# Fixed step patterns, earlier k turns and spread loads in a threshold-attention kernel followed by a tanh-shrink layer

## The chip, the cores and the metric

The kernel runs on one core of a Trainium2 chip. The metric is device time in microseconds (us), lower is better. A core has TensorE (PE in the profile, matmuls), VectorE (DVE), ScalarE (ACT), GpSimd (POOL) and SyncE (SP, which here issues nearly all transfers). Each engine works off its own instructions in order and waits on semaphores for the others. PSUM is the memory that PE writes; only DVE and ACT read it here.

## The reference

```python
# q, k, v: 8 batches x 8 heads x 576 rows x 64, float32; tau = 0.02
scores = scale * np.matmul(q, k.transpose(0, 1, 3, 2))
thresh = np.max(scores, axis=-1, keepdims=True) - tau
scores = np.where(scores >= thresh, scores, -1000000000.0)
attn = softmax(scores)                   # written out in the reference
attn_out = np.matmul(attn, v)
x = attn_out.transpose(0, 2, 1, 3).reshape(4608, 512)
h = x @ w_in                             # 512 x 2048
out = (h - np.tanh(h)) @ w_out           # 2048 x 512
```

## The kernel before

**Pairs, tiles, slots.** Two heads of one batch make a pair p (32 pairs, 0 to 31; four pairs are a batch). A pair has nine tiles of 128 query rows (288 in all). One loop over a slot number s, from -8 to 292, writes the whole program: slot s issues the scores of tile s + 8, the threshold of tile s + 5, the exponentials of tile s and the value products of tile s - 2, so that every tile passes through all engines over some ten slots. Nothing reorders the code afterwards. The order of the loop is the order on each engine.

**What a slot holds.** On PE: the scores `psS` (two matmuls of 512 columns and two of 64, lines 322 and 331), then in some slots a layer step, in every odd slot the value products `psO` (lines 425, 432, 443), and what the plan adds. On DVE: the copy `sc` out of the scores with the row maximum (341), in every second slot `nb` (353), then `g` (517), `rc` and `osb` (457 to 463, the division by the sum), `xT` and `xR` (488, 489). On ACT: `z` (368), `th` (511, the tanh), and in every second slot `pT` (404, the exponential for two tiles). From pair 6 on the transposition between `z` and `pT` is a DMA, `zT`, issued by SP in every even slot (line 375); before that it is done on PE (`psZ`, 387).

**Layer steps.** When a batch is done, its 512 main rows go through the layer in a stage: 16 h steps (`psH`, four matmuls of 512 columns against w_in, line 498) and 16 y steps (`psY`, four matmuls of 512 columns against w_out, line 524; four parts make one output tile, copied out by `yo`, line 537, and stored by SP). Stage m runs beside the attention of batch m + 1, in the 36 slots from slot 36(m + 1) + 4; the last, for batch 6, has 32. `layers` makes the list of steps, and a running share spreads it evenly over `room`, the slots without a turn of k: 32 steps in 32 slots. Two stages follow after the last slot, at one step after another. The first stage has 16 h steps and 3 y steps.

**Turns and loads (the plan).** k and q of a pair are loaded as float32 (`kraw`, `qraw`, `vraw`; two DMAs each), split on POOL into two halves (`khl`, `qhl`), and turned: nine PE transposes into PSUM (`ps_k`, `ps_q`, line 240) and a copy by DVE (`kT`, `qT`, line 263). For k, POOL then copies the halves crosswise into `kS` (two copies of 64 x 1152, line 269), which the scores need as well. From pair 8 on q of three pairs in four is turned by a DMA instead (`qT<-qhl`, line 252). `PREP` says how many slots ahead of the pair's first scores (which are issued in slot 9p - 8) each of these stands. From pair 5 on k is turned six slots ahead for odd p and three for even p, in a slot that has no layer step. Loads of k, q and v stand in three slots in a row.

**PSUM.** `ps_big` has two buffers of two banks each, shared in turn by the scores of every tile and by the turns `ps_k` and `ps_q`: the third such tile has to wait until the first is copied out. `ps_h` has two buffers (h steps, `psX`), `ps_y` one (`psY`), `ps_o` one (`psO`).

Of the kernel before, what the change touches and what calls it, by code (L numbers as in the profile page):

```python
# [9 lines left out]
F32 = mybir.dt.float32  # L10
# [8 lines left out]
def kernel(  # L19
# [12 lines left out]
    P = 128  # L32

    B, H, S, D = q.shape
# [11 lines left out]
    HPAIR = H // 2  # L46
    NPAIR = B * HPAIR
# [4 lines left out]
    TPP = 9  # L52
    NTILE = NPAIR * TPP
# [9 lines left out]
    AHEAD = 8  # L63
    LDK = 16
# [61 lines left out]
    ps_big = pool("ps_big", 2, space=PSUM)  # L126
    ps_o = pool("ps_o", 1, space=PSUM)
# [108 lines left out]
    def turn_chunk(out, c, lhsT):  # L236
# [4 lines left out]
            out=out, lhsT=lhsT, rhs=rhs, is_transpose=True, start=True, stop=True  # L241
        )

    def q_by_dma(p):

        return p >= 2 * HPAIR and p % 4 != 0
# [49 lines left out]
    scs, mxs, nbs, zs, zts, pts, ops = {}, {}, {}, {}, {}, {}, {}  # L296

    def kind(i):

        return "AB"[i % 2]  # L300

    def place(i):

        p, j = divmod(i, TPP)
        j = j - p % 2
        return (p, None, 4) if j in (-1, 8) else (p, j // 4, j % 4)
# [102 lines left out]
    def attend(i):  # L409

        if kind(i) == "A":
            return
        p, hh, t = place(i)
        vb, pt = vbs[p % NV], pts[i]
        if hh is None:

            attend_shared(p - 1, 0, pt)
            return
        if t == 1:
            ops[p, hh] = ps_o.tile([P, 6, D + 1], F32, name="psO", tag="o")  # L420
            if p % 2 and hh == 0:
                attend_shared(p, 1, pts.pop(i - 2))
        po = ops[p, hh]

        nc.tensor.matmul(  # L425
            out=po[:, t - 1 : t + 1, :], lhsT=pt[:, 4 * P : 5 * P],
            rhs=vb[:, hh, 4:6, :], start=True, stop=False, skip_group_check=True,
        )
        for n in range(8):
            ab, c = divmod(n, 4)  # L430
            blk = 5 * ab + c
            nc.tensor.matmul(  # L432
                out=po[:, t - 1 + ab, :], lhsT=pt[:, blk * P : (blk + 1) * P],
                rhs=vb[:, hh, c, :], start=False, stop=(n == 7), skip_group_check=True,
            )
        pts.pop(i)
# [70 lines left out]
    def bend():  # L507
        while halves:
            m, n, ps = halves.pop(0)
            th = t_pool.tile([P, MB], F32, name="th")  # L510
            nc.scalar.activation(out=th, in_=ps, func=ACT.Tanh)  # L511
            ths.append((m, n, ps, th))
# [40 lines left out]
    EARLY = lambda m: 3 if m else 3  # L553
    LAST = 1

    FIRST = 3
    quarters = lambda m: [(m, ms, part) for ms in range(4) for part in range(4)]

    def layers(m, tail):


        def h_step(n):
            if tail and n % 2:
                ps = ps_big.tile([P, MB], F32, name="psHt", tag="big")
            else:
                ps = ps_h.tile([P, MB], F32, name="psH", tag="h")
            hidden(m, n, ps)

        def y_step(m, ms, part):
            if part == 0:  # L570

                odd = tail and (m, ms) > (B - 2, 1) and ms % 2 == 0
                pl, tag = (ps_o, "o") if odd else (ps_y, "y")
                ys[m, ms] = pl.tile([P, d_model], F32, name="psY", tag=tag), odd
            ps, odd = ys[m, ms]
            project(m, ms, part, ps, odd)

        def y_half(h):

            n = d_model // 2  # L580
            pl, tag = ((ps_y, "y"), (ps_o, "o"))[h]
            ps = pl.tile([P, n], F32, name="psY", tag=tag)
            for part in range(4):
                project(m, 3, part, ps, h == 0, slice(h * n, h * n + n))

        now = quarters(m - 1)[EARLY(m - 1) :] if m > 0 else []
        if m < NMB - 1:
            now += quarters(m)[: EARLY(m)]
        else:
            now += quarters(m)[:12]  # L590
        n = 16 + len(now)


        ahead = n - max(0, EARLY(m) - 3) - LAST if m < NMB - 1 else n - 9 - LAST
        steps, at, i = [], [], 0

        def ready(y):
            last = 4 * y[2] + 3
            return y[0] < m or len(at) > (last if m else 15) and at[last] + 2 < i

        while now or len(at) < 16:
            if len(at) < 16 and (
                not now or not ready(now[0]) or len(at) * ahead <= i * 16
            ) and not (m == B - 1 and i < FIRST):
                steps.append(lambda a=len(at): h_step(a))
                at.append(i)
            elif ready(now[0]):
                steps.append(lambda y=now.pop(0): y_step(*y))
            else:
                steps.append(lambda: None)  # L610
            i += 1
        if m == NMB - 1:
            steps += [lambda h=h: y_half(h) for h in range(2)]
        return steps
# [44 lines left out]
    for p in range(1, NPAIR):  # L659
        first = TPP * p - AHEAD  # L660
        for d, f in PREP[3 if p == 1 else 0 :]:
            d -= p == 1 and d in (3, 5)
            if d in (7, 8) and q_by_dma(p):
                d = d + 2
            if p in (2, 4):
                d = {8: 9, 7: 8, 5: 6}.get(d, d)
            elif d == 5 and p >= 5:
                d = 6 if p % 2 else 3
            plan.setdefault(first - d, []).append(lambda p=p, f=f: f(p))
        d = 7 if q_by_dma(p) else 3 - (p == 1 or p >= 5)  # L670
        d = 4 if p in (2, 4) else d
        plan.setdefault(first - d, []).append(lambda p=p: turn(p, "q"))

# [14 lines left out]
    todo, stage = [], 0  # L688
# [4 lines left out]
            plan.setdefault(-AHEAD, []).extend(plan.pop(at))  # L693

    turns = set()
    for p in range(HPAIR + 1, NPAIR):
        d = 6 if p % 2 else 3
        turns.add(TPP * p - AHEAD - (d if p >= 5 else 5))  # L700

    kinks, wts, atts = {}, {}, {}
    for i in range(NTILE + 3):
        at = i - 4 if i < HPAIR * TPP else i
# [4 lines left out]
    for s in range(-AHEAD, NTILE + LAG + 3):  # L709
        p, j = divmod(max(s, 0), TPP)  # L710
        if 0 <= s < NTILE and j == 2 + LAG and p % HPAIR == 0 and p >= HPAIR:
            assert not todo
            todo = layers(stage, False)
            room = range(s, min(s + HPAIR * TPP, NTILE))
            if room[-1] + 1 < NTILE:
                room = [a for a in room if a not in turns]
            share = len(todo) / len(room)
            done, stage = 0.0, stage + 1
        if s == NTILE:
            todo = layers(stage, True)  # L720
            share, done, stage = 1, 0.0, stage + 1
        if 0 <= s + AHEAD - 1 < NTILE:
            shift(s + AHEAD - 1)

        n = s + AHEAD
        if 0 < n < NTILE and place(n)[1] is None and kind(n) == "B":
            scores(n - 1)
        if 0 <= n < NTILE and (place(n)[1] is not None or kind(n) == "B"):
            scores(n)
        if s == 1 - AHEAD:  # L730
            for t in ("k", "q", "ks"):
                turn_first(t, 1)
        for i in kinks.pop(s, []):
            kink(i)
        bend()
        for i in wts.pop(s, []):
            weights(i)
        if 0 <= s < NTILE + FIRST:
            if todo and (s >= NTILE or s in room):
                done += share  # L740
                if s < NTILE and s == room[-1]:
                    done = 1e9
                while todo and done >= 1:
                    todo.pop(0)()
                    done -= 1
        if s == 0:
            nc.vector.tensor_tensor(
                out=fold, in0=ident_bf[:, 0:64], in1=ident_bf[:, 64:P], op=ALU.add
            )
        shrink()  # L750
        for store in stores[:-1]:
            store()
        del stores[:-1]
        for i in atts.pop(s, []):
            pp, jj = divmod(i, TPP)
            if i < NTILE:
                attend(i)
                odd = pp % 2
                if jj == 3 + odd:
                    norm(pp, 0)  # L760
                elif odd and jj in (0, 8):
                    norm(pp - (jj == 0), 1)
            if pp and jj == 1 + pp % 2:
                emit_x(pp - 1)
        for step in plan.pop(s, []):
            step()
        if s + AHEAD in cast_when:
            w_cast()
        if s + AHEAD in load_when:
            w_load(next(pieces))  # L770

    for step in todo:
        step()
        bend()
        shrink()
        for store in stores:
            store()
        stores.clear()
# [10 lines left out]
    _ = bass_utils  # L789
# [35 lines left out]
```

## Time and profile before

| | |
|---|---|
| median of 3 runs | 531.35 us (531.02 to 531.88) |
| the profiled execution's own time | 532.69 us |
| its span, first to last instruction | 530.9 us |
| busy: PE, ACT, DVE, POOL | 507.7, 433.4, 422.1, 289.3 us |
| TensorE clock granted | 1.0 of full speed throughout |
| DMA queue of SP | 85.56 MB, 77.4% of 16 engines' span |

The profile comes from one execution. A row of the timeline has the start in us, the duration, the engine and line, the operation with the tile it writes and those it reads, and in brackets how long the engine had stood idle before it and whose instruction ended that. Matmul ends are modelled: a row of PE ends about 0.16 us after the next one can start, so that a hole in PE is about that much longer than the idle time in brackets.

### The profile page before, as it was taken

How to read it: one execution, taken by the hardware profiler on the slowest of the kernel's cores; microseconds unless marked ns; L12 is line 12 of the kernel's file. 1: busy time of each engine (PE TensorE's matmuls, PEld its weight loads, DVE VectorE, ACT ScalarE, POOL GpSimd, SP SyncE). 2: the span in 40 equal slices, each digit the busy share in tenths (PEclk: the TensorE clock that was granted, in tenths of full speed). 3: DMA queues.
4: the chain of work that ended last, by engine and by line, in shares of the span. 5: the costliest groups of instructions: out<-in, count | busy, mean ns of one | idle time of the engine just before them, and what ended most of it. 6: DMA issues, size and time to landing. Idle time of an engine off the chain costs nothing.

```text
span 530.9 us, 12707 instructions
## 1 busy us (share of the span) xinstructions
PE 507.7 (96%) x4606; PEld 286.4 (54%) x4606; DVE 422.1 (80%) x1179; ACT 433.4 (82%) x617; POOL 289.3 (54%) x390
## 2 busy tenths in 40 slices
PE   8999899989999989999999999999999999999996
PEld 4666566554555545555555555555555555444444
DVE  5999889997898878998889888888899887554440
ACT  5999999998898989988998989899998989544330
POOL 7999999684738366574738383846657430000000
PEclk9999999999999999999999999999999999999999
DMA  7843668989799999899998999999988976400113
GB/s 215 242 141 112 216 214 168 184 145 201 180 199 162 183 181 202 167 193 205 180 198 180 199 175 216 157 198 185 204 169 196 202 133 110 105 36 25 39 41 80
DMA packets 208607, 86.79 MB, mean 163 GB/s; under 512 B 176160, under 2 KB 200992, under 8 KB 208544
## 3 DMA queue, kind: packets, MB, share of 16 engines
q1 hardware_dynamic: 207952, 85.56, 77.4%
q8 instruction: 36, 0.59, 0.5%
q10 hardware_dynamic: 592, 0.43, 0.3%
q14 instruction: 27, 0.22, 0.1%
HBM read 36.70 MB, written 9.44 MB: 87 GB/s over the span
## 4 chain that ended last, share of the span: by engine, by line
PE 48%; issue 13%; ACT 12%; DVE 12%; POOL 7%; DMA 7%; SPq 1%; ACTq 0%; POOLq 0%; DVEq 0%
PE psY L524 15%; PE psH L498 12%; PE psS L331 9%; ACT z L368 5%; DVE sc L341 4%; ACT pT L396 3%; DMA zT<-z 3%; PE psHt L498 3%; DVE g L517 2%; PE psO L432 2%; ACT th L511 2%; POOL kS L269 2%; ACT pT L404 2%; DMA vraw<-in_v_dram 2%; PE psS L322 2%
## 5 line engine op out<-in xcount | busy, mean ns | idle before, releaser
L341 DVE TENSOR_SCALAR_CACHE_REDUCE sc<-psS 128x576 f32<-128x576 f32 x288 | 212.9, 753 | 34.2 <-PE psS L331 21.3
L368 ACT ACTIVATE z<-sc,nb 128x576 bf16<-128x576 f32 x288 | 216.0, 769 | 27.6 <-DVE nb L353 27.1
L524 PE MATMUL psY<-w_out_sb,g 128*128 128x512 bf16 (+1 forms) x592 | 146.0, 374 | 0.8 <-DVE yo L537 0.8
L404 ACT ACTIVATE pT<-zT 128x1152 f16<-128x1152 bf16 x117 | 135.0, 1154 | 10.6 <-DMA zT<-z 10.4
L269 POOL COPY kS<-kT 64x1152 f16<-64x1152 f16 x62 | 70.8, 1142 | 125.4 <-DVE nb L353 123.7
L498 PE MATMUL psH<-xT,w_in_sb 128*128 128x512 bf16 x480 | 123.3, 379 | 0.7 <-DVE g L517 0.3
L331 PEld LDWEIGHTS <-qT 128*128 128x128 f16 x1024 | 75.1, 97 | 67.3 <-issue 11.8
L331 PE MATMUL psS<-kT,qT 128*128 128x512 f16 (+1 forms) x512 | 104.3, 285 | 7.2 <-DVE sc L341 4.0
L517 DVE SCALAR_TENSOR_TENSOR g<-th,psH 128x512 bf16<-128x512 f32 x128 | 87.6, 684 | 25.5 <-ACT th L511 23.6
L331 PE MATMUL psS<-kS,qT 128*128 128x512 f16 x496 | 101.3, 286 | 1.7 <-POOL kS L269 1.6
L511 ACT ACTIVATE th<-psH 128x512 f32<-128x512 f32 x128 | 74.6, 583 | 21.9 <-PE psH L498 21.8
L524 PEld LDWEIGHTS <-g 128*128 128x128 bf16 x592 | 51.0, 98 | 57.2 <-issue 3.5
L498 PEld LDWEIGHTS <-w_in_sb 128*128 128x128 bf16 x576 | 48.8, 98 | 53.2 <-issue 1.0
L432 PE MATMUL psO<-vb,pT 128*128 128x65 bf16 x1024 | 53.3, 194 | 0.0
L432 PEld LDWEIGHTS <-pT 128*128 128x128 f16 x1024 | 44.2, 98 | 9.4
L193 POOL TENSOR_TENSOR khl<-kraw,khl 128x576 f16<-128x576 f32 x31 | 39.7, 1281 | 2.6
L193 POOL TENSOR_TENSOR qhl<-qraw,qhl 128x576 f16<-128x576 f32 x31 | 39.7, 1280 | 2.6
L396 ACT ACTIVATE pT<-psZ 128x512 f16<-128x512 bf16 (+1 forms) x54 | 35.1, 654 | 2.6 <-PE psZ L387 2.1
L537 DVE COPY yo<-psY 128x512 f32<-128x512 f32 (+1 forms) x31 | 21.1, 682 | 13.6 <-PE psY L524 12.4
L458 DVE TENSOR_TENSOR osb<-psO,rc 128x256 bf16<-128x256 f32 x64 | 27.2, 424 | 2.2
L425 PE MATMUL psO<-vb,pT 128*128 128x130 bf16 x128 | 28.1, 220 | 0.6 <-DVE nb L353 0.6
L387 PE MATMUL psZ<-ident_bf,z 128*128 128x128 bf16 x243 | 22.5, 220 | 2.1 <-ACT pT L396 1.3
(79 smaller groups left out, 509.5 us busy)
## 6 DMA issues: line engine op xcount, KB each, us to landing
vraw<-in_v_dram SPq DMA_DIRECT2D x32, 256.0 KB, 3.6
out_dram<-yo SPq DMA_DIRECT2D x32, 256.0 KB, 3.1
kraw<-in_k_dram SPq DMA_DIRECT2D x31, 256.0 KB, 3.1
qraw<-in_q_dram SPq DMA_DIRECT2D x31, 256.0 KB, 3.4
wt<-in_moe_w_in_dram SPq DMA_DIRECT2D x8, 512.0 KB, 4.6
wt<-in_moe_w_out_dram SPq DMA_DIRECT2D x8, 512.0 KB, 4.2
zT<-z SPq DMA_TRANSPOSE x117, 3.7
qraw<-in_q_dram SPq DMA_DIRECT2D x32, 32.0 KB, 3.1
```

The costliest lines, as they stand in the source:

```text
L193: nc.gpsimd.tensor_tensor(out=hl[:, :, 1, :], in0=x, in1=hl[:, :, 0, :], op=ALU.subtract)
L269: nc.gpsimd.tensor_copy(out=o, in_=i)
L331: nc.tensor.matmul(out=ps[:, dst], lhsT=lhs, rhs=kk[:, src], start=(n == 0), stop=(n == 1),)
L341: nc.vector.tensor_scalar(out=sc, in0=ps[:, lo : lo + S], scalar1=SC, scalar2=None, op0=ALU.mult, op1=ALU.max, accum_out=mx[:, c : c + 1],)
L368: nc.scalar.activation(out=z, in_=sc, func=ACT.Prelu, bias=nb, scale=1.0, alpha=STEEP)
L396: nc.scalar.activation(out=pt[:, off * P : (off + n) * P], in_=ps[:, 0 : n * P], func=ACT.Exp)
L404: nc.scalar.activation(out=pt[:, 0 : n * P], in_=zts.pop(i)[:, 0:n, :], func=ACT.Exp)
L432: nc.tensor.matmul(out=po[:, t - 1 + ab, :], lhsT=pt[:, blk * P : (blk + 1) * P], rhs=vb[:, hh, c, :], start=False, stop=(n == 7), skip_gr ...
L498: nc.tensor.matmul(out=ps, lhsT=w_in_sb[:, c, n * P : (n + 1) * P], rhs=xs[m][:, c, :] if m < B else xR[:, c, :, :], start=(c == 0), stop= ...
L511: nc.scalar.activation(out=th, in_=ps, func=ACT.Tanh)
L517: nc.vector.scalar_tensor_tensor(out=gs[m][:, n, :], in0=th, scalar=-1.0, in1=ps, op0=ALU.mult, op1=ALU.add,)
L524: nc.tensor.matmul(out=ps, lhsT=gs[m][:, n, ms * P : (ms + 1) * P], rhs=w_out_sb[:, n, cols], start=(n == 0), stop=(n == DF_C - 1),)
```

## The change

1. Each stage inside the attention gets a written pattern, one character per slot: h, y, or - for a slot without a step. `room`, `turns` and the running share go. The first stage's pattern puts its steps into the same slots as before, and the stage of batch 6 alternates h and y as before.
2. k is turned six slots ahead for every pair from 5 on, also where a step stands (`k_lead`). For odd p this is the slot it had; for even p it was three slots later. In the stages of batches 1 to 5 all four turns of k now have a step beside them; the four slots of such a stage without a step are the 8th, 18th, 25th and 32nd.
3. Loads of k, q and v of pairs from 5 on stand in every second slot, in slots in which no `zT` is issued, and q of odd pairs is turned by DMA one slot later.
4. The value products of the last pair, and the first output tile of batch 6, use `ps_big` instead of `ps_o` and `ps_y`.
5. A y step may follow its h step one slot sooner (`ready`); the two stages at the end come out in the same order.

```diff
             out=out, lhsT=lhsT, rhs=rhs, is_transpose=True, start=True, stop=True
         )
 
+    def k_lead(p):
+        if p < HPAIR + 2:
+            return 6 if p in (2, 4) or p == HPAIR + 1 else 5 - (p == 1)
+        return (6, 6)[1 - p % 2]
+
     def q_by_dma(p):
 
         return p >= 2 * HPAIR and p % 4 != 0
...
             attend_shared(p - 1, 0, pt)
             return
         if t == 1:
-            ops[p, hh] = ps_o.tile([P, 6, D + 1], F32, name="psO", tag="o")
+
+            pl, tag = (ps_big, "big") if p == NPAIR - 1 else (ps_o, "o")
+            ops[p, hh] = pl.tile([P, 6, D + 1], F32, name="psO", tag=tag)
             if p % 2 and hh == 0:
                 attend_shared(p, 1, pts.pop(i - 2))
         po = ops[p, hh]
...
     EARLY = lambda m: 3 if m else 3
     LAST = 1
 
+    PATTERN = lambda m: '-h--h-hh--h-hh-h-hh-h--hh-h--hh-y-yy' if m == 0 else 'hyhyhyhyhyhyhyhyhyhyhyhyhyhyhyhy' if m == B - 2 else 'yhyhyyy-yhyhhyyhy-hhhyhh-hyhyhy-yhhy'
+
     FIRST = 3
     quarters = lambda m: [(m, ms, part) for ms in range(4) for part in range(4)]
 
-    def layers(m, tail):
+    def layers(m, tail, pattern=None):
 
 
         def h_step(n):
...
 
                 odd = tail and (m, ms) > (B - 2, 1) and ms % 2 == 0
                 pl, tag = (ps_o, "o") if odd else (ps_y, "y")
+                if (m, ms) == (B - 2, 0):
+                    pl, tag = ps_big, "big"
                 ys[m, ms] = pl.tile([P, d_model], F32, name="psY", tag=tag), odd
             ps, odd = ys[m, ms]
             project(m, ms, part, ps, odd)
...
 
         def ready(y):
             last = 4 * y[2] + 3
-            return y[0] < m or len(at) > (last if m else 15) and at[last] + 2 < i
+            return y[0] < m or len(at) > (last if m else 15) and at[last] + 1 < i
+
+        if pattern is not None:
+            for i, kind in enumerate(pattern):
+                for one in kind:
+                    if one == "h":
+                        steps.append((i, lambda a=len(at): h_step(a)))
+                        at.append(i)
+                    elif one == "y":
+                        assert ready(now[0]), (m, i, now[0])
+                        steps.append((i, lambda y=now.pop(0): y_step(*y)))
+            assert not now and len(at) == 16, (m, now, len(at))
+            return steps
 
         while now or len(at) < 16:
             if len(at) < 16 and (
...
     for p in range(1, NPAIR):
         first = TPP * p - AHEAD
         for d, f in PREP[3 if p == 1 else 0 :]:
-            d -= p == 1 and d in (3, 5)
-            if d in (7, 8) and q_by_dma(p):
-                d = d + 2
-            if p in (2, 4):
-                d = {8: 9, 7: 8, 5: 6}.get(d, d)
-            elif d == 5 and p >= 5:
-                d = 6 if p % 2 else 3
+            d -= p == 1 and d == 3
+            if p > HPAIR and d >= LDK - 2:
+                d = ((16, 14, 12), (17, 15, 13))[1 - p % 2][LDK - d]
+            elif d in (7, 8) and q_by_dma(p):
+                d = ((9, 9) if d == 7 else (10, 10))[1 - p % 2]
+            elif d == 4:
+                d = 4
+            elif d == 5:
+                d = k_lead(p)
+            elif p in (2, 4):
+                d = {8: 9, 7: 8}.get(d, d)
             plan.setdefault(first - d, []).append(lambda p=p, f=f: f(p))
-        d = 7 if q_by_dma(p) else 3 - (p == 1 or p >= 5)
+        d = (6, 7)[1 - p % 2] if q_by_dma(p) else 3 - (p == 1 or p >= 5)
         d = 4 if p in (2, 4) else d
         plan.setdefault(first - d, []).append(lambda p=p: turn(p, "q"))
 
...
             plan.setdefault(-AHEAD, []).extend(plan.pop(at))
 
 
-
-    turns = set()
-    for p in range(HPAIR + 1, NPAIR):
-        d = 6 if p % 2 else 3
-        turns.add(TPP * p - AHEAD - (d if p >= 5 else 5))
-
     kinks, wts, atts = {}, {}, {}
     for i in range(NTILE + 3):
         at = i - 4 if i < HPAIR * TPP else i
...
         p, j = divmod(max(s, 0), TPP)
         if 0 <= s < NTILE and j == 2 + LAG and p % HPAIR == 0 and p >= HPAIR:
             assert not todo
-            todo = layers(stage, False)
-            room = range(s, min(s + HPAIR * TPP, NTILE))
-            if room[-1] + 1 < NTILE:
-                room = [a for a in room if a not in turns]
-            share = len(todo) / len(room)
-            done, stage = 0.0, stage + 1
+            todo = [(s + i, step) for i, step in layers(stage, False, PATTERN(stage))]
+            stage += 1
         if s == NTILE:
-            todo = layers(stage, True)
-            share, done, stage = 1, 0.0, stage + 1
+            todo = [(s + n, step) for n, step in enumerate(layers(stage, True))]
+            stage += 1
         if 0 <= s + AHEAD - 1 < NTILE:
             shift(s + AHEAD - 1)
 
...
         bend()
         for i in wts.pop(s, []):
             weights(i)
-        if 0 <= s < NTILE + FIRST:
-            if todo and (s >= NTILE or s in room):
-                done += share
-                if s < NTILE and s == room[-1]:
-                    done = 1e9
-                while todo and done >= 1:
-                    todo.pop(0)()
-                    done -= 1
+        while todo and todo[0][0] <= s < NTILE + FIRST:
+            todo.pop(0)[1]()
         if s == 0:
             nc.vector.tensor_tensor(
                 out=fold, in0=ident_bf[:, 0:64], in1=ident_bf[:, 64:P], op=ALU.add
```

How the instructions stand. The first place is DVE around the turn of k of pair 16, in the stage of batch 2 (`kT` and `qT` are the copies of turned k and q, `sc` that of scores, `g` the layer's, `nb` the thresholds, `rc` and `osb` the division, `xT` and `xR` the copies of a finished pair). Before:

```order
L341 TENSOR_SCALAR sc,mx_101<-psS 128x576 x2
L517 SCALAR_TENSOR_TENSOR g<-th,psH 128x512
L263 COPY kT<-ps_k 128x1152
L353 TENSOR_SCALAR nb<-mx_101 128x3x2
L341 TENSOR_SCALAR sc,mx_103<-psS 128x576
L263 COPY qT<-ps_q 128x1152
L341 TENSOR_SCALAR sc,mx_103<-psS 128x576
L353 TENSOR_SCALAR nb<-mx_103 128x3x2
```

The copy of k stood between two scores' copies, one slot ahead of the copy of q. Now:

```order
L495 COPY xT<-psX 128x512
L496 CAST xR<-psX 128x64
L358 TENSOR_SCALAR nb<-mx_97 128x3x2
L346 TENSOR_SCALAR sc,mx_99<-psS 128x576
L268 COPY kT<-ps_k 128x1152
L346 TENSOR_SCALAR sc,mx_99<-psS 128x576
L524 SCALAR_TENSOR_TENSOR g<-th,psH 128x512
L464 RECIPROCAL rc<-psO 128x4
L465 TENSOR_TENSOR osb<-psO,rc 128x4x64
```

The copy of k has moved three slots up, between the copies of two scores right behind those of a finished pair (`xT`, `xR`), and the copy of q, which has stayed in its slot, no longer follows it.

The second place is SP in the stage of batch 2, from the DMA turn of q of pair 14 on (`zT` is the transposition that `pT` on ACT needs). Before:

```order
L252 DMA_TRANSPOSE qT<-qhl 128x9x128
L145 DMA kraw<-in_k_dram 128x2x256
L153 DMA kraw<-in_k_dram 128x1x64
L375 DMA_TRANSPOSE zT<-z 128x9x128
L145 DMA qraw<-in_q_dram 128x2x256
L153 DMA qraw<-in_q_dram 128x1x64
L540 DMA out_dram<-yo 128x512
L145 DMA vraw<-in_v_dram 128x2x256
L151 DMA vraw<-in_v_dram 64x2x64
L375 DMA_TRANSPOSE zT<-z 128x9x128 x4
```

Two loads and a store stood between one `zT` and the next. Now:

```order
L257 DMA_TRANSPOSE qT<-qhl 128x9x128
L145 DMA kraw<-in_k_dram 128x2x256
L153 DMA kraw<-in_k_dram 128x1x64
L380 DMA_TRANSPOSE zT<-z 128x9x128
L547 DMA out_dram<-yo 128x512
L145 DMA qraw<-in_q_dram 128x2x256
L153 DMA qraw<-in_q_dram 128x1x64
L380 DMA_TRANSPOSE zT<-z 128x9x128
L145 DMA vraw<-in_v_dram 128x2x256
L151 DMA vraw<-in_v_dram 64x2x64
L380 DMA_TRANSPOSE zT<-z 128x9x128 x2
```

A `zT` now stands between the load of q and that of v, and the store comes earlier.

More of the change, by code (lines that the diff above doesn't have):

```diff
@@ L770 @@
             w_load(next(pieces))
-    for step in todo:
+    for _, step in todo:
         step()
```

## The prediction

> **What bounds the kernel now.** I read the table of windows first, then PE's waits in that window, then the timeline around each kind of wait. The window from 117 to 426 us holds the five middle stages and most of the sixth.
>
> ```profile
> span 530.9 us, 12707 instructions
> 117.00:426.00 309.00, 301.43 (x2734) 167.64 (x2733) 267.91 (x759) 275.19 (x374) 182.35 (x234) 1.00 0.97 187
> 463.67 0.86 PE psHt L498 x4
> 464.53 0.86 PE psH L498 x4
> PE psS L331 <- DVE sc L341: 2.9, 3, 1.2
> PE ps_k L240 <- DVE sc L341: 1.8, 10, 0.2
> PE psS L331 <- POOL kS L269: 1.6, 5, 0.3
> PE psO L425 <- DVE nb L353: 0.6, 1, 0.6
> ```
>
> The window's row gives PE 301.4 busy of 309 us, DVE 267.9, ACT 275.2, POOL 182.4. The next two rows, from the chain in the tail, show PE at its own pace: a step of four 512-column matmuls every 0.86 us, 0.216 us each. PE sets the time, and its work does not change, so the change can win only what PE waits. The last four rows are all those waits in the window: 6.9 us printed, in 19 holes.
>
> The holes are longer than printed. Rows of PE overlap the next start:
>
> ```profile
> 186.55 2.33 POOL L269 COPY kS<-kT 64x1152 f16<-64x1152 f16 x2 [8.70 <-DVE nb L353]
> 188.20 0.41 PE L331 MATMUL psS<-kT,qT 128*128 128x512 f16 x2
> 188.93 0.41 PE L331 MATMUL psS<-kS,qT 128*128 128x512 f16 x2 [0.32 <-POOL kS L269]
> 190.03 0.41 PE L331 MATMUL psS<-kT,qT 128*128 128x512 f16 x2
> 190.28 0.41 PE L331 MATMUL psS<-kS,qT 128*128 128x512 f16 x2
> ```
>
> Undisturbed, the second half of a score starts 0.25 us after the first (190.03, 190.28), each printed with 0.41: an overlap of 0.16. At 188.93 it starts 0.73 late instead, a hole of 0.49 behind a printed 0.32. I add 0.16 to each printed idle time.
>
> In the Trainium skill, "TensorE: Matmul & The Clock Gate", section "Back-to-back issue gap", a stream of 512-column matmuls is given a sustained 131 ns each, and about 216 ns only for one alone. The trace disagrees: 216 ns each in a stream. By the page a step would be an estimated 0.52 us, PE would mostly be waiting for something else, and the third rival below would be the forecast.
>
> **The change, part by part.** No instruction is added or removed on any engine; they move.
>
> *Turns of even k* (pairs 10 to 28, slots without a step). The rows are those of pair 16, the place that the order shows:
>
> ```profile
> 213.78 0.41 PE L432 MATMUL psO<-vb,pT 128*128 128x65 bf16 x8
> 214.24 0.75 DVE L341 TENSOR_SCALAR_CACHE_REDUCE sc<-psS 128x576 f32<-128x576 f32 x1
> 214.37 0.66 PE L240 MATMUL ps_k<-ident_f,khl 128*128 128x128 f16 x9 [0.17 <-DVE sc L341]
> 215.03 0.69 DVE L517 SCALAR_TENSOR_TENSOR g<-th,psH 128x512 bf16<-128x512 f32 x1
> 215.05 0.41 PE L331 MATMUL psS<-kT,qT 128*128 128x512 f16 x2
> 215.54 1.03 PE L524 MATMUL psY<-w_out_sb,g 128*128 128x512 bf16 x4
> 215.64 0.75 DVE L263 COPY kT<-ps_k 128x1152 f16<-128x1152 f16 x1
> 216.37 0.75 DVE L341 TENSOR_SCALAR_CACHE_REDUCE sc<-psS 128x576 f32<-128x576 f32 x1
> 216.44 0.66 PE L240 MATMUL ps_q<-ident_f,qhl 128*128 128x128 f16 x9
> 217.18 0.41 PE L331 MATMUL psS<-kT,qT 128*128 128x512 f16 x2
> ```
>
> The turn waits for a score bank: 0.17 + 0.16 = 0.33. The next score follows at 215.05 where 214.37 + 0.66 - 0.16 = 214.87 was due, 0.18 more. With a step between, PE works 0.86 us longer before the turn, more than the sum of both, so 0.51 goes at each of ten turns: **5.1 us**. On DVE the copy of 0.75 us goes into slots that now hold no `g` of 0.69; PE covers the turn's own bank with a score and a step, 0.49 + 0.86 us, before the next but one score needs it. Behind the turn of q (five times) the score starts at 217.18 where 216.94 was due, because the copy of k delayed the score's copy; that copy is gone from there: 5 x 0.24 = **1.2 us**.
>
> *`kS` six slots ahead.* POOL stood idle 8.70 us for the turn and then finished too late for the first score. Three more slots hold three scores of 0.49 and at least two steps of 0.86, over 3 us, against a hole of 0.49; five of them, **2.4 us**. POOL's next splits stand behind `kS` in its queue and come earlier too.
>
> *Turns of odd k and the loads.* Their slot is the same; the step beside is new, and the loads have moved.
>
> ```profile
> 185.34 0.53 SPq L540 DMA_DIRECT2D out_dram<-yo  x1
> 185.92 0.43 SPq L145 DMA_DIRECT2D vraw<-in_v_dram  x1
> 187.14 5.47 SPq L375 DMA_TRANSPOSE zT<-z  x3
> 192.53 1.16 ACT L404 ACTIVATE pT<-zT 128x1152 f16<-128x1152 bf16 x1 [2.19 <-DMA zT<-z]
> 194.87 0.69 DVE L517 SCALAR_TENSOR_TENSOR g<-th,psH 128x512 bf16<-128x512 f32 x1 [1.34 <-ACT th L511]
> 195.78 1.31 SPq L252 DMA_TRANSPOSE qT<-qhl  x1
> 196.29 0.41 PE L331 MATMUL psS<-kT,qT 128*128 128x512 f16 x2 [1.25 <-DVE sc L341]
> 250.41 1.16 ACT L404 ACTIVATE pT<-zT 128x1152 f16<-128x1152 bf16 x1 [1.41 <-DMA zT<-z]
> 254.18 0.41 PE L331 MATMUL psS<-kT,qT 128*128 128x512 f16 x2 [0.47 <-DVE sc L341]
> ```
>
> This is a chain: a `zT` issued behind a store and loads lands late, ACT stands 2.19 us, its tanh is late, so DVE's `g`, so the score's copy queued behind it, and PE stands 1.25 + 0.16. The second case gives 0.63 for 1.41 of ACT's wait. Both times PE's hole is the wait less 0.78. A step of 0.86 us beside the turn raises this cushion to 1.64, and the loads now stand between transposes instead of in a row. I take the 2.9 + 3 x 0.16 = 3.4 us as gone, and half of the 0.6 + 0.16 at `psO`, which waits for a `pT` too: **3.8 us**. The bounds are 2.3 (the cushion alone: 2.19 - 1.64 = 0.55 is left of the hole of 1.41, and at most as much of a second) and 4.1.
>
> *First stage.* The steps stay; the turn of pair 8 moves from a bare slot to one with a step.
>
> ```profile
> 97.91 0.66 PE L240 MATMUL ps_k<-ident_f,khl 128*128 128x128 f16 x9 [0.18 <-DVE sc L341]
> 99.92 0.66 PE L240 MATMUL ps_q<-ident_f,qhl 128*128 128x128 f16 x9 [0.68 <-DVE kT L263]
> 100.66 0.41 PE L331 MATMUL psS<-kT,qT 128*128 128x512 f16 x2
> ```
>
> The holes here are 0.34, 0.18, 0.84 and 0.24, 1.6 together. The turn of q stays in a bare slot and, like the even turns, will find DVE busy; I leave it 0.7 and take **0.9 us**. The turn of pair 6 goes to another bare slot: nothing, 0.4 at most.
>
> *Last pair in the score banks.*
>
> ```profile
> 453.54 0.45 PE L443 MATMUL psO<-vb,pT 128*128 128x130 bf16 x5 [0.28 <-DVE osb L463]
> 453.65 0.69 DVE L517 SCALAR_TENSOR_TENSOR g<-th,psH 128x512 bf16<-128x512 f32 x1 [0.26 <-ACT th L511]
> 454.39 1.03 PE L498 MATMUL psH<-xT,w_in_sb 128*128 128x512 bf16 x4
> 459.53 0.69 DVE L537 COPY yo<-psY 128x512 f32<-128x512 f32 x1 [0.72 <-PE psY L524]
> 460.28 1.02 PE L524 MATMUL psY<-w_out_sb,g 128*128 128x512 bf16 x4 [0.78 <-DVE yo L537]
> ```
>
> The wait for `yo` goes, since the next tile has its own bank: 0.94. The wait for `osb` of 0.44 goes too, but the h step at 454.39 needs the `g` that ends at 453.65 + 0.69 = 454.34 and would be due at 453.95: 0.39 comes back. **1.0 us**.
>
> *What may be late next.* Four slots of each middle stage have no step now; there PE has 0.86 us less cover for the score's copy. The turns in bare slots, which had 0.5 us more of PE work but also a third user of the banks, lost 0.51. I find no bare slot that is also a turn in these stages, and put 1 us in all against them and against the three h steps in a row (range 0 to 7).
>
> Sum: 5.1 + 1.2 + 2.4 + 3.8 + 0.9 + 1.0 - 1.0 = 13.4 us. The profiled execution took 532.69 us for its span of 530.9, 1.8 around it, and stands 1.3 above the median of 531.35. Span 517.5, own time 519.3, on the median's scale **518.0 us**.
>
> **The rivals.** *Late transposes stay.* The loads still stand directly ahead of the next `zT`, one pair instead of two and a store. If that is enough to keep them as late as before, and the cushion does not help, the 3.8 us stay: 521.8. Against it speaks the second case above, where ACT's wait was 0.78 shorter and so was PE's. The Trainium skill, "DMA: Bandwidth & Descriptors", section "Queues, rings and completion order", says that each DMA engine takes a queue's descriptors in ring order; by that rule a transpose waits for whatever was issued before it, this rival's mechanism, and the late row at 187.14 agrees.
>
> *Bare slots take over the waits.* With PE's 13 us gone, ACT's 275.2 us fall into 296, 93%, and DVE's 267.9 into 90%. If each of the 20 bare slots in the middle stages costs the 0.33 us of a bank that is not free, 6.6 us come back: 524.6.
>
> *PE does not set the pace.* If ACT did, PE's holes would only move: 531, no change. Against it: ACT stands idle 33.8 us of the window, PE 7.6.
>
> *Slower.* q of the 12 odd pairs from 9 on is turned by DMA one slot later, between two loads: SP issues it in 1.31 us and a load in 0.43 or more (185.92), and the next `zT` stands behind all of it. Should that make a `zT` 1.31 us later than the worst before, ACT stands 3.5 us, PE 3.5 - 1.64 = 1.9 at each, 22 in all: 540. It decides from 1.2 us per pair, an ACT wait of 2.8, since 13.4 are won elsewhere. Against it: this turn stood between `zT` and loads before as well.
>
> **How the numbers follow.** Forecast 0.62, late transposes 0.14, bare slots 0.12, no change 0.04, slower 0.05, anything else 0.03. A difference under 0.2% (1.1 us) cannot be told from none here. Faster 0.90, within 0.2% 0.04, slower 0.06. The forecast's own range is 515.5 (no new holes, all of the chain gone, the first stage without holes) to 520.5; the range reaches up over the first two rivals: 514.5 to 525.5.
>
> **What the profile would show.** Right: no wait of `ps_k` or `psS` for `sc` around the turns in the middle stages, none for `kS`, the wait before `psY` at the end of the attention gone, PE over 99% busy there. ACT's wait for `zT` well under 10 us if the loads were its cause; the same 10 us with few holes in PE if the step beside the turn is what helps. Wrong: waits of `psS` for `sc` behind slots without a step, of `psH` for `g` in the three h steps, or of `psO` for `pT`; or a span that shrinks by less than PE's waits do.

## The result and the profile after

| | before | after |
|---|---|---|
| median of 4 runs each | 531.62 us (531.02 to 532.03) | 518.01 us (518.00 to 518.02) |
| ratio, 95% interval | | 0.9745 [0.9728, 0.9762] |
| the profiled execution's own time | 532.69 us | 518.02 us |
| its span | 530.9 us | 516.2 us |

The change takes 13.6 us off the medians and 14.7 us off the two profiled spans; the profiled execution of before stood 1.1 us above its median, that of after on it.

First the span, the shares of the chain that ended last, and the table of windows of the kernel after. 117 to 413 us holds the slots that stood in 117 to 426 us before. The columns of a window's row are its length, then busy time and records of PE, weight loads, DVE, ACT and POOL, the granted clock, the DMA share and GB/s.

```profile
span 516.2 us, 12626 instructions
PE 77%; POOL 9%; ACT 4%; DVE 3%; issue 3%; DMA 2%; SPq 1%; POOLq 0%; ACTq 0%; DVEq 0%
117.00:413.00 296.00, 292.78 (x2694) 166.50 (x2739) 265.20 (x760) 274.77 (x374) 182.81 (x233) 1.00 1.02 194
```

The same shares of the chain before:

```profile
PE 48%; issue 13%; ACT 12%; DVE 12%; POOL 7%; DMA 7%; SPq 1%; ACTq 0%; POOLq 0%; DVEq 0%
```

13.0 of the 14.7 us lie in this window: 309 us became 296. Nothing lies ahead of it (the kernel stands at slot 76 after 119.5 us before, 119.4 after), and the rest at the end. The chain, half of which was waits and work of other engines, is now mostly PE. PE's busy time reads 98.9%, but the window has 2694 records of matmuls for 2739 weight loads: 45 are missing here. Two rows of the table of waits of the kernel after, the first in this window, the second over the whole span, and then the row of the kernel before that answers to the second:

```profile
PE psH L505 <- issue: 1.0, 6, 0.2
ACT pT L409 <- DMA zT<-z: 1.4, 4, 0.6
ACT pT L404 <- DMA zT<-z: 10.4, 12, 2.2
```

The first is the only row that PE has there, where before it had four, and its six places are such missing records. ACT's wait for `zT` (total, times, longest) fell from 10.4 us in 12 places to 1.4 in 4.

The turn of k of pair 16, now beside an h step, from the timeline of the kernel after:

```profile
202.64 0.41 PE L336 MATMUL psS<-kS,qT 128*128 128x512 f16 x2
202.89 1.03 PE L505 MATMUL psH<-xT,w_in_sb 128*128 128x512 bf16 x4
203.75 0.67 PE L240 MATMUL ps_k<-ident_f,khl 128*128 128x128 f16 x9
204.26 0.41 PE L336 MATMUL psS<-kT,qT 128*128 128x512 f16 x2
204.50 0.41 PE L336 MATMUL psS<-kS,qT 128*128 128x512 f16 x2
204.53 0.76 DVE L268 COPY kT<-ps_k 128x1152 f16<-128x1152 f16 x1 [0.47 <-PE ps_k L240]
204.75 1.03 PE L505 MATMUL psH<-xT,w_in_sb 128*128 128x512 bf16 x4
205.20 0.75 DVE L346 TENSOR_SCALAR_CACHE_REDUCE sc<-psS 128x576 f32<-128x576 f32 x1
205.87 0.68 DVE L524 SCALAR_TENSOR_TENSOR g<-th,psH 128x512 bf16<-128x512 f32 x1
206.17 0.41 PE L336 MATMUL psS<-kS,qT 128*128 128x512 f16 x2
206.61 1.02 PE L505 MATMUL psH<-xT,w_in_sb 128*128 128x512 bf16 x3
```

The turn starts 0.86 us after the step does (202.89, 203.75), and the next score 0.51 later (204.26): no hole in front of either, and no brackets. The last row is the one new hole: the score's second half at 206.17 leaves PE free 0.25 us later, at 206.42, and the third h step of a row starts at 206.61. Its bank comes free with the `g` that ends at 205.87 + 0.68 = 206.55; `g` stands behind the copy of the score, and that behind the copy of k. This hole of 0.2 stands once in each of the five middle stages (151.02, 206.61, 262.19, 317.78 and 373.37 us), 1.0 us in all. Nothing of it is printed, since the modelled end of the row ahead covers 0.16 of it.

The first stage, where nothing was won (holes of 1.6 us before, 1.7 after), in the timeline of the kernel after:

```profile
98.48 0.41 PE L336 MATMUL psS<-kT,qT 128*128 128x512 f16 x2 [0.17 <-DVE sc L346]
99.16 0.66 PE L240 MATMUL ps_q<-ident_f,qhl 128*128 128x128 f16 x9
99.75 0.75 DVE L346 TENSOR_SCALAR_CACHE_REDUCE sc<-psS 128x576 f32<-128x576 f32 x1
100.56 0.41 PE L336 MATMUL psS<-kT,qT 128*128 128x512 f16 x2 [0.74 <-DVE sc L346]
109.79 0.41 PE L336 MATMUL psS<-kT,qT 128*128 128x512 f16 x2 [1.20 <-DVE kT L268]
```

`ps_q` no longer waits 0.68 us, but the score behind it now waits 0.74 for the score's copy at 99.75. The wait at 109.79 stood there before too.

And the end of the attention:

```profile
440.29 0.69 DVE L524 SCALAR_TENSOR_TENSOR g<-th,psH 128x512 bf16<-128x512 f32 x1 [0.25 <-ACT th L518]
441.03 1.02 PE L505 MATMUL psH<-xT,w_in_sb 128*128 128x512 bf16 x3 [0.27 <-DVE g L524]
445.11 1.89 PE L531 MATMUL psY<-w_out_sb,g 128*128 128x512 bf16 x8
```

The two output tiles now follow each other in one run of eight matmuls (8 x 0.216 + 0.16 = 1.89): the wait for `yo` of 0.94 is gone. That for `osb` is gone too and came back as the wait of `psH` for `g`, 0.27 + 0.16.

### The profile page after: what moved, and what is told of

Read it like the earlier page. It is cut to its first block, busy times and chain, and to the rows that moved or that the text cites. A ratio compares the mean times of both kernels' runs of the same rounds, so it can differ in the third digit from the quotient of the medians.

```text
span 516.2 us, 12626 instructions
## 1 busy us (share of the span) xinstructions
PE 497.8 (96%) x4540; PEld 285.3 (55%) x4606; DVE 418.8 (81%) x1179; ACT 432.8 (84%) x617; POOL 290.2 (56%) x390
## 4 chain that ended last, share of the span: by engine, by line
PE 77%; POOL 9%; ACT 4%; DVE 3%; issue 3%; DMA 2%; SPq 1%; POOLq 0%; ACTq 0%; DVEq 0%
PE psY L531 22%; PE psH L505 19%; PE psS L336 18%; PE psO L439 5%; PE psS L327 3%; PE psHt L505 3%; PE ps_k L240 3%; POOL kS L274 2%; DMA kraw<-in_k_dram 2%; POOL w_in_sb L655 1%; PE psO L450 1%; ACT pT L409 1%; POOL khl L193 1%; PE psO L432 1%; ACT z L373 1%
## 5 line engine op out<-in xcount | busy, mean ns | idle before, releaser
L531 PE MATMUL psY<-w_out_sb,g 128*128 128x512 bf16 (+1 forms) x565 | 140.2, 373 | 1.3 <-issue 0.2
L505 PE MATMUL psH<-xT,w_in_sb 128*128 128x512 bf16 x443 | 117.8, 379 | 3.5 <-issue 1.1
L336 PEld LDWEIGHTS <-qT 128*128 128x128 f16 x1024 | 72.9, 97 | 56.5 <-issue 5.5
L544 DVE COPY yo<-psY 128x512 f32<-128x512 f32 (+1 forms) x31 | 21.1, 681 | 14.7 <-PE psY L531 13.8
L268 DVE COPY kT<-ps_k 128x1152 f16<-128x1152 f16 x31 | 23.4, 756 | 4.4 <-PE ps_k L240 4.3
```

The lines of the kernel that those rows point to most:

```text
L336: nc.tensor.matmul(out=ps[:, dst], lhsT=lhs, rhs=kk[:, src], start=(n == 0), stop=(n == 1),)
L505: nc.tensor.matmul(out=ps, lhsT=w_in_sb[:, c, n * P : (n + 1) * P], rhs=xs[m][:, c, :] if m < B else xR[:, c, :, :], start=(c == 0), stop= ...
L531: nc.tensor.matmul(out=ps, lhsT=gs[m][:, n, ms * P : (ms + 1) * P], rhs=w_out_sb[:, n, cols], start=(n == 0), stop=(n == DF_C - 1),)
```

## The experiments

Times are medians of four runs; differences are to the kernel after (518.01 us) unless said otherwise. Ratios are to the kernel before, run on the same chip, with their 95% interval. The kernel after was not run again beside them; up to where the first changed instruction stands, the traces agree with its own to 0.1 us, so that the small differences can be read. A hole is counted from start to start, so that its 0.16 is in it.

**1. The loads in a row again, all else as after** (loads_in_a_row).

```diff
-                d = ((16, 14, 12), (17, 15, 13))[1 - p % 2][LDK - d]
+                pass
```

> The changed kernel with its loads of k, q and v back in three slots in a row. If the step beside the turn of k (a cushion of 0.86 us) is what hides a late transposition, at most the 1.1 us that the cushion leaves come back: 518.0 to 519.2 us, with ACT's wait for zT back near 10 us. If the spread of the loads is what took those holes away, the 3.8 us booked for them come back: about 521.8 us.

519.47 us (518.38 to 519.83), ratio 0.9769 [0.9744, 0.9794]: 1.46 us slower. Its group of `pT` on ACT (busy time and mean ns, then the idle time before it and how much of that one releaser ended), and rows of its timeline at a late `zT`:

```profile
L409 ACT ACTIVATE pT<-zT 128x1152 f16<-128x1152 bf16 x117 | 135.1, 1155 | 18.7 <-DMA zT<-z 17.3
314.78 0.69 DVE L524 SCALAR_TENSOR_TENSOR g<-th,psH 128x512 bf16<-128x512 f32 x1 [1.18 <-ACT th L518]
315.52 1.02 PE L505 MATMUL psH<-xT,w_in_sb 128*128 128x512 bf16 x4 [0.44 <-DVE g L524]
317.40 0.41 PE L336 MATMUL psS<-kT,qT 128*128 128x512 f16 x2 [0.35 <-DVE sc L346]
```

ACT waits 17.3 us for `zT`, more than before the change (why more is not shown), in an execution of 519.83 us, 1.8 above the kernel after. At PE's worst place, the turn of k of pair 24, the chain of the prediction is seen again (ACT late by 1.6, `th` late, `g` late), and PE loses 0.60 and 0.51. ACT's four longest waits, 2.0 to 2.4 us, cost PE nothing. So the loads make `zT` late, and the steps beside the turns cover most of it.

Where a `zT` loses its time can be read at the worst one of the kernel before:

```profile
182.76 0.76 ACT L368 ACTIVATE z<-sc,nb 128x576 bf16<-128x576 f32 x1
184.04 0.61 SPq L145 DMA_DIRECT2D qraw<-in_q_dram  x1
186.40 0.64 SPq L151 DMA_DIRECT2D vraw<-in_v_dram  x1
187.14 1.78 SPq L375 DMA_TRANSPOSE zT<-z  x1
```

The second `z` of its two tiles is ready at 183.52. SP then issues four loads and a store, from 184.04 to 187.04, and the transpose after them: 3.6 us behind its `z`, where the median of all 117 is 0.8. It lands 5.3 us after that, where the median is 3.7. So the larger part of the delay, 2.8 of 4.4 us over the medians, is there before the transpose is issued. The ring-order rule of the Trainium skill ("DMA: Bandwidth & Descriptors", "Queues, rings and completion order"), that a DMA engine takes the descriptors of a queue in order, could bear on the rest, the later landing; no run here shows whether it does.

**2. Only the spread loads, in the kernel before** (spread_loads_alone).

```diff
-            if d in (7, 8) and q_by_dma(p):
+            if p > HPAIR and d >= LDK - 2:
+                d = ((16, 14, 12), (17, 15, 13))[1 - p % 2][LDK - d]
+            elif d in (7, 8) and q_by_dma(p):
```

> The kernel before with only its loads moved into every second slot. If loads in a row make the transpositions late, ACT's wait for zT falls from 10 us to under 3 and PE's holes behind it go: 527.5 to 528.5 us. If the transpositions are late for another reason (the store, the DMA turn of q), no change: 531.0 to 531.9 us.

527.65 us (527.61 to 527.70), ratio 0.9926 [0.9899, 0.9953]: 3.6 us under the kernel before (531.26 beside it). Its waits:

```profile
ACT pT L404 <- DMA zT<-z: 1.3, 2, 0.7
PE ps_k L240 <- DVE sc L341: 1.9, 11, 0.2
PE psS L331 <- POOL kS L269: 1.6, 5, 0.3
```

The wait of 10.4 us is down to 1.3 without any step beside a turn (a `zT` is now issued 0.3 us behind its `z` in the median), and PE's waits for a bank at the turns and for `kS` stand as they were. The loads alone carry the term for late transposes.

**3. The turns of k back into slots without a step, all else as after** (bare_turns). The four slots without a step of a middle stage become those of the four turns.

```diff
-'yhyhyyy-yhyhhyyhy-hhhyhh-hyhyhy-yhhy'
+'-yhyhyyyh-yyhhyyhy-hhyhhyhh-yhyhyhhy'
```

> The changed kernel with another pattern in the five middle stages: the turns of k stay six slots ahead, but in slots without a step; the 32 steps go to the other slots, and no three h steps stand in a row. If the step beside the turn covers the score bank, 0.33 + 0.18 us come back at each of ten turns of even k and something at the odd ones, less 1.0 for the missing row of three: 521.5 to 524 us. If the six slots and the spread loads are what wins, 517 to 518.2 us.

526.76 us (526.69 to 526.82), ratio 0.9909 [0.9887, 0.9932]: 8.75 us slower, more than expected. One row of its waits over the whole span, and its timeline at the same turn as above:

```profile
PE psS L336 <- DVE sc L346: 7.6, 17, 0.7
205.48 0.42 DVE L495 COPY xT<-psX 128x512 bf16<-128x512 bf16 x1
205.49 0.67 PE L240 MATMUL ps_k<-ident_f,khl 128*128 128x128 f16 x9
206.01 0.75 DVE L346 TENSOR_SCALAR_CACHE_REDUCE sc<-psS 128x576 f32<-128x576 f32 x1
206.82 0.41 PE L336 MATMUL psS<-kT,qT 128*128 128x512 f16 x2 [0.66 <-DVE sc L346]
```

With the step gone, the score behind the turn needs the bank whose copy starts only at 206.01, behind `xT` and its neighbours on DVE: a hole of 0.82. I had reckoned with the 0.51 of before; at six slots the turn stands right behind a finished pair, and the hole is larger (0.83, 0.56), with 0.2 to 0.3 more at each odd turn. The ten even turns add to 6.9 and the ten odd ones to 2.4; less the 1.0 of the third h steps, which is gone, that is nearly all of the 8.75. The step beside the turn is the largest part of the change. Experiments 2 and 3 lie 0.9 us apart, the size of the banks' term (experiment 5): without the steps the six slots bring nothing in all.

**4. k of even pairs three slots ahead, steps and all else as after** (even_k_three_ahead).

```diff
-        return (6, 6)[1 - p % 2]
+        return (6, 3)[1 - p % 2]
```

> The changed kernel with k of even pairs turned three slots ahead again; in this pattern both slots have a step, so only the distance changes. If the distance matters, the first score waits for kS again (2.4 us) and the turn of q stands behind the copy of k again (up to 1.2 us): 520.4 to 521.6 us. If the step beside is all that counts, 517.9 to 518.5 us.

518.60 us (518.51 to 518.71), ratio 0.9756 [0.9734, 0.9778]: 0.59 us slower. Its timeline at the first scores of pair 14:

```profile
182.64 2.33 POOL L274 COPY kS<-kT 64x1152 f16<-64x1152 f16 x2 [7.85 <-DVE nb L358]
184.56 0.41 PE L336 MATMUL psS<-kT,qT 128*128 128x512 f16 x2
185.02 0.41 PE L336 MATMUL psS<-kS,qT 128*128 128x512 f16 x2
```

`kS` makes PE late by 0.21 (185.02, due 0.25 after 184.56) where it was 0.49, and the hole behind the turn of q does not come back. This stands at six pairs (10, 14, 18, 22, 26 and 30), 1.3 us in all, while the holes of 0.2 at the third h steps shrink to 0.04, which gives 0.8 back. The distance, to which the prediction gave 3.6 us, is worth 1.3 by itself and 0.6 on balance; the step beside the turn does most of its work.

**5. The last pair in its own banks again, all else as after** (last_pair_own_banks).

```diff
-            pl, tag = (ps_big, "big") if p == NPAIR - 1 else (ps_o, "o")
+            pl, tag = ps_o, "o"
...
-                if (m, ms) == (B - 2, 0):
-                    pl, tag = ps_big, "big"
```

> The changed kernel with the last pair's value products and the first output tile of batch 6 back in their own banks. By the prediction's sum the wait for yo (0.94 us) comes back and that for osb nearly not: 519.0 us. If the chain of the last pair hides it, 518.0 us.

518.95 us (518.95 to 519.05), ratio 0.9772 [0.9745, 0.9799]: 0.94 us slower. Its timeline has both waits of before:

```profile
440.27 0.45 PE L450 MATMUL psO<-vb,pT 128*128 128x130 bf16 x5 [0.27 <-DVE osb L470]
447.01 1.02 PE L531 MATMUL psY<-w_out_sb,g 128*128 128x512 bf16 x4 [0.78 <-DVE yo L544]
```

**6. Two steps of the first stage moved, slot 63 to 62 (the turn of q) and slot 66 to 67** (first_stage_steps).

```diff
-'-h--h-hh--h-hh-h-hh-h--hh-h--hh-y-yy'
+'-h--h-hh--h-hh-h-hh-h-h-h--h-hh-y-yy'
```

> The changed kernel with other slots for five of the 16 h steps of the first stage: one stands beside the turn of q of pair 8 and one beside the turn of k of pair 9, both bare before. The changed kernel has holes of 1.7 us at each of the two places. If the missing step is their cause, 514.6 to 516.2 us. If DVE or ACT is simply full there, the holes move a few slots on: 517.6 to 518.4 us.

The pattern moves two steps, not the five of the expectation. 517.18 us (517.14 to 517.24), ratio 0.9738 [0.9712, 0.9765]: 0.83 us faster, where 2 to 3 were expected. Its timeline:

```profile
106.45 0.47 PE L450 MATMUL psO<-vb,pT 128*128 128x130 bf16 x5 [0.65 <-DVE nb L358]
108.99 0.41 PE L336 MATMUL psS<-kT,qT 128*128 128x512 f16 x2 [0.48 <-DVE kT L268]
```

The holes of 0.90 and 1.36 shrink to 0.23 and 0.65, but the value products then wait 0.81 instead of 0.33 (the row at 106.45). Part of what PE waits for here came late in both orders.

**7. No three h steps in a row** (no_three_h), and **8. both patterns** (both_patterns).

```diff
-'yhyhyyy-yhyhhyyhy-hhhyhh-hyhyhy-yhhy'
+'yhyhyyy-yhyhhyyhy-hhyhh-hhyhyhy-yhhy'
```

> The changed kernel with no three h steps in a row in the middle stages (a y step stands third, and a bare slot one earlier). Five holes of 0.2 us of the third h step, which waits for the g of the first, should go: 517.0 us. If DVE is full there, the hole shows up at the next wait: 518.0 us.

> Both new patterns, that of the first stage and that of the middle stages. If the two gains add: 513.6 to 515.2 us. If both were only shifts: 518.0 us.

518.36 us (518.19 to 518.69), ratio 0.9761 [0.9734, 0.9789], and 517.51 us (517.46 to 517.83), ratio 0.9747 [0.9714, 0.9779]: 0.35 slower and 0.50 faster. The five holes of 0.2 at the third h step go, and another takes the place of each, where a score waits for the copy of q: 0.66 in the first stage of the five and 0.21 in the other four (timeline of no_three_h; the value products ahead of the score leave PE free at 212.16):

```profile
211.56 0.76 DVE L268 COPY qT<-ps_q 128x1152 f16<-128x1152 f16 x1
212.37 0.42 PE L336 MATMUL psS<-kT,qT 128*128 128x512 f16 x2
```

Both edits add up (0.83 - 0.35 = 0.48). This left open what makes the 0.2: three h steps in a row, or where the copy of k stands on DVE.

**9. On experiment 6: even k five slots ahead** (five_ahead), and **10. four** (four_ahead).

```diff
-        return (6, 6)[1 - p % 2]
+        return (6, 5)[1 - p % 2]
```

> The kernel of first_stage_steps (517.18 us) with k of even pairs turned five slots ahead instead of six. What is asked: where do the five holes of 0.20 us come from that PE has before the third h step of a row in each middle stage? Theory: the copy of k on DVE (0.75 us) stands ahead of the g that this step's bank waits for; one slot later it stands behind that g, the five holes go, and kS is still over 1.4 us early, since at three slots it is late by only 0.215 us: 516.2. Rival: the three h steps in a row are the cause by themselves (two banks, one of them also taken by psX), wherever the copy of k stands: the holes stay, 517.2. Second rival: the copy of k now delays another bank, as the copy of q did in no_three_h with 0.215 us a stage: 517.2 with the holes at another place.

> The kernel of first_stage_steps (517.18 us) with k of even pairs turned four slots ahead instead of six. By the theory of five_ahead the five holes of 0.20 us go here too; kS would have one slot (some 1.6 us) more than at three slots, where it was late by 0.215 us, so none of it shows: 516.2, the same as five slots. If it is three h steps in a row as such: 517.2. If kS is late again because POOL has other work in that slot, up to 5 x 0.215 come back: 517.2 with kS holes.

517.19 us (517.03 to 517.27), ratio 0.973 [0.9712, 0.9748], and 518.56 us (518.25 to 518.91), ratio 0.9756 [0.9734, 0.9778]: neither is the 516.2 that was expected. With five slots all five holes are gone, but pairs 12 and 30 pay 0.35 and 0.59 behind their turns. With four slots, four of the holes shrink to 0.04 and the one of pair 12 grows to 0.83; 0.42 and 1.07 come in near the turn of pair 10, and 0.66 at that of pair 30, while the stretch around pair 8 gets 0.7 shorter. Why these pairs pay was not followed up.

**11. On experiment 6: five slots for pairs 16, 20, 24 and 28 alone** (five_for_four_pairs).

```diff
-        return (6, 6)[1 - p % 2]
+        return 5 if p % 4 == 0 and p >= 16 else 6
```

> The kernel of first_stage_steps (517.18 us) with k of pairs 16, 20, 24 and 28 alone turned five slots ahead; all others stay at six. In five_ahead the holes of 0.20 us at the third h step were gone, but the turns of pairs 12 and 30 then cost 0.35 and 0.59 us elsewhere. If the place of k's copy on DVE is what makes the 0.20 us, four of the five holes go and nothing else changes: 517.18 - 0.8 = 516.4. If the gain of five_ahead came from another of its pairs, or if the loss at pair 12 is that of any first pair with five slots and only moves to pair 16: 516.8 to 517.2.

516.40 us (516.38 to 516.45), ratio 0.9707 [0.9667, 0.9746], as expected. Its timeline at the third h step of pair 16's turn:

```profile
204.38 0.68 DVE L524 SCALAR_TENSOR_TENSOR g<-th,psH 128x512 bf16<-128x512 f32 x1
205.33 0.41 PE L336 MATMUL psS<-kS,qT 128*128 128x512 f16 x2
205.53 0.74 DVE L268 COPY kT<-ps_k 128x1152 f16<-128x1152 f16 x1
205.57 1.03 PE L505 MATMUL psH<-xT,w_in_sb 128*128 128x512 bf16 x3
```

The same three h steps stand in a row, but the copy of k comes behind `g`, and the third starts on time (205.57, 0.24 after the score). So the holes of 0.2 came from the place of k's copy on DVE. Moving the copy pays at these four pairs, not everywhere (experiments 9 and 10). This version beats both kernels: it is 1.6 us under the one after, 0.8 of it by experiment 6.

## Why the prediction was right, and where its terms were off

518.0 was forecast and 518.01 measured. Experiment 2 splits the way in two: from the kernel before (531.26) the spread loads take 3.6, to 527.65; the rest of the change takes 9.64, to 518.01. The terms, as they were booked:

| term | booked | measured |
|---|---|---|
| turns of odd k and the loads | 3.8 | 3.6 by the loads alone |
| turns of even k, turn of q, `kS` | 5.1 + 1.2 + 2.4 = 8.7 | about 9.8 (9.64 less the three rows below) |
| first stage | 0.9 | -0.1 |
| last pair in the score banks | 1.0 | 0.94 |
| new waits | -1.0 | -1.0 at the third h steps |

*What held.* PE set the pace, and the holes in which it waits for another engine are gone from the middle: 1.0 us is left of 296. (Gaps of 0.09 ahead of and behind each score issued by line 327 stood there before as well.) The named waits went as forecast: `ps_k` and `psS` for `sc`, `kS`, `yo`; `osb` came back as `g`. Of the signs of being wrong, one showed, the wait of `psH` for `g` in the three h steps, at the size that had been set aside for it. DVE and ACT now work 265.2 and 274.8 of the 296 us, as full as the rival of bare slots supposed (90% and 93%), and the bare slots still cost nothing: no hole stands at one. The case of slower by q's turn between two loads did not occur, since ACT waits 1.4 us in all.

*The cause of late transposes.* The prediction left open whether the loads or the step beside the turn would help, and named the sign for each. It was the loads: the sign was ACT's wait, 1.4 us. Each covers most of the wait alone, and that is why they do not add: the loads are worth 3.6 us without the steps and 1.46 with them. The difference of 2.1 is what the step's cushion saves; the prediction's lower bound, "the cushion alone", was 2.3. The rival with late transposes at 521.8 was wrong about the price: with ACT's wait back, 17.3 us in the profiled execution, the kernel takes 519.47. But the cushion is not the fixed 1.64 of the prediction: in experiment 1 waits of 2.0 to 2.4 us cost PE nothing, and one of 1.6 cost 1.1. And where this rival counts one pair of loads left ahead of a `zT`, the order of SP after the change shows a store and a pair at one place.

*Terms credited to the wrong part.* The 2.4 for `kS` and the 1.2 for q were put down to six slots instead of three. (The prediction's "0.73 late" at 188.93 is the distance from the first half; late it is by the 0.49 that the sum uses.) With three slots and the step left in place, the distance is worth 0.59 on balance, and 1.3 for `kS` alone. The step beside the turn gives the time: taking it away costs 8.75 (experiment 3; at six slots the bare turns have longer holes than before, so the number is not the booked 5.1 measured again).

*The first stage.* Booked 0.9, measured nothing. The step was "the turn of pair 8 moves from a bare slot to one with a step": it did, and the wait of `ps_q` went, but DVE is behind there, and the score after `ps_q` waits instead.

*The sum.* By pieces it is 3.6 + 9.8 - 0.1 + 0.94 - 1.0 = 13.2 against 13.4: 1.0 too much in the first stage, 1.1 too little at the turns. The 9.8 is what is left over, not a count. The period of a middle stage gives nearly as much: from one turn to the same turn of the next stage 57.27 us in experiment 2 (239.51 to 296.78) and 55.58 after (206.61 to 262.19), so 1.69 x 5 is won net, and 9.5 with the 1.0 of the third h steps added back. The trace of experiment 2 has the holes that were booked at 8.7 in full (3.4 + 1.8 at the even turns, 1.2 behind the turns of q, 2.4 for `kS`); beside them 0.2 stands at `kS` of pair 30 and 0.6 in 17 holes under 0.1 each, which the prediction did not list. That makes 9.5 as well; the last 0.3 is open. The sum fits the medians; between the two profiled spans it is 1.3 short (14.7), as much as the profiled execution of before stood above the median it was set against, a surplus that the one after no longer has.

*Luck.* The way was right, but the agreement to 0.01 us is luck. The two errors of the sum cancel, the 1.0 set aside for new waits was a round figure out of a range of 0 to 7, and taking 1.3 off for the profiled execution made up for the 1.3 by which the sum falls short of the spans.

## What to carry to other kernels

When one engine sets the pace, a list of its holes from one start to the next can price a change of order, as it did here, but each hole goes to the credit of whatever covers it first: remove the covers one at a time before crediting a part. A third user of a pair of score banks belongs beside long work of the engine that fills them, not into an empty slot, and the copy that frees the bank should stand behind, not ahead of, a copy for which that engine waits next; try such a move at each place, since here it paid at four pairs and cost as much at two others. Transfers that a nearly full engine waits for should alternate with bulk loads in the order of the engine that issues them, rather than stand behind a row of them.

## What was not expected of the hardware

The scatter of the times went with the loads in a row. The kernel before took 529.38 to 533.53 us over all its runs here, and with the loads in a row and the steps beside the turns it was 518.38 to 519.83; the kernel after took 518.00 to 518.02, and that of experiment 2, 527.61 to 527.70. Variants with spread loads but longer waits of ACT for `zT` scattered a little more (four_ahead: 4.4 us of waiting, 518.25 to 518.91). Another does not fit: no_three_h scattered by 0.50 with 1.8 us of waiting. That late transposes differ from run to run may be the cause; it was not shown.
